# Where seven Strassen products stand between the tiles of second products in an attention, experts and MLP kernel

## The chip, the cores and the metric

The kernel runs on one core of a Trainium2 chip. The metric is the device time of one execution in microseconds; three runs of a kernel are timed and their median is compared. One further execution is recorded by the hardware profiler; its rows are in microseconds from the start of its span unless marked ns.

## The reference

Three layers follow each other on 1152 tokens of 512 features. First an attention (2 batches, 8 heads, 576 positions, head size 64) that adds a coarse softmax attention over groups of four positions to a local one over the seven nearest positions. Then a mixture of eight experts whose weights P come from a gate and eight Sinkhorn rounds. Then an MLP with a softplus.

```python
out_up = np.repeat(out_d, factor, axis=2)       # coarse attention
x = out_up + out_local                          # (1152, 512)
logits = x @ w_gate; P = np.exp(logits - logits.max())
for _ in range(8):                              # Sinkhorn
    P /= P.sum(1, keepdims=True) + 1e-09
    P /= P.sum(0, keepdims=True) + 1e-09
    P *= N / E
for e in range(8):                              # w1: 512x1024, w2: 1024x512
    out += P[:, e:e+1] * (np.maximum(x @ w1[e], 0) @ w2[e])
h = out @ w_in                                  # 512 x 2048
return (np.maximum(h, 0) + np.log1p(np.exp(-np.abs(h)))) @ w_out
```

## The kernel before, in words

The MLP is treated as two more experts, so there are ten (`NE`), numbered 0 to 9. Tokens are split in two sets: s=0 holds 512 (four tiles of 128, halves of 256), s=1 holds 640 (five tiles, halves of 320). An expert's hidden width is cut in four pairs of 128-row blocks (`p`). One step is one expert, one token set and one `p`; there are 80 steps, listed in `steps`. Steps 0 to 3 run beside the attention, steps 4 to 79 afterwards in the main loop (line 792).

**First products.** `first(n)` computes a step's hidden values by a Strassen scheme: seven products (lines 623 to 648) in the order 4, 0, 2, 5, 1, 3, 6 instead of eight. All arithmetic is fp32 split in a high and a low part (`xh`, `xl`, `w1h`, `w1l`), so each product is six matmuls (line 601) of 256 or 320 columns. Products 4, 2, 1 and 6 use one PSUM bank in turn, products 0 and 3 share a second bank, product 5 has a third, which is the first bank of the next step. Therefore product 2 waits until ScalarE has copied product 4 out (`t1`, line 610), product 1 until product 2 is copied (`u2`), product 6 until VectorE has added product 1 into `c22` (line 615), and the next step's product 5 until the hidden values of product 6 (`hh` by ScalarE, line 558, and `hl` by VectorE, line 559, both read from the bank) are made. In the MLP steps the hidden values take a longer chain (lines 563 to 575).

**Second products.** `second(n, ...)` multiplies one token tile of the hidden values with `w2`: six matmuls of 512 columns (line 660) into the tile's own PSUM bank. After the last step of a group, `weigh` (line 677) adds the bank into `acc` on VectorE.

**Order of the work.** TensorE's order is the order in which the program emits its instructions (`manual_schedule`). The other engines' orders are planned by a list scheduler from the same program. In the usual step n of the main loop the seven products of step n+2 (`ahead[n] == [n + 2]`) are shared out ahead of the tiles of second products of step n. With four tiles the shares are 2, 2, 2, 1, with five tiles 2, 2, 1, 1, 1. Of the 76 steps of the main loop 68 are usual ones (4 to 57 and 64 to 77): 30 have four tiles and 38 five. Around the turn from experts to MLP (58 to 63) other shares hold, and the last two steps have no products.

**What else hangs on the order.** `lead(n)` calls `fetch_first` once a weight block has been used for the last time: after product 6 its buffers are refilled, with two DMAs into `raw` (issued on SyncE), casts on ScalarE (lines 132 and 138), sums on GpSimd (line 111) and low parts on VectorE and GpSimd (lines 133 and 139). For experts 1 to 6 this is the case in each four-tile step: 24 times. For the MLP's blocks the refill is two DMAs alone. `used(n)` does the same for `w2` after the last tile. `convert` (32 pieces, from step 12) turns the MLP's float64 weights into split fp32 on VectorE, ScalarE and GpSimd. Up to step 8 a piece of the Sinkhorn rounds (`next(balance)`) follows each tile but the first; every second one begins with a small matmul (line 509) that waits for VectorE.

Of the kernel before, what the change touches and what calls it, by code (L numbers as in the profile page):

```python
# [20 lines left out]
def attention_moe_mlp(ctx: ExitStack, tc: tile.TileContext, q, k, v, w_gate, w1, w2, w_in, w_out, out):  # L21
# [3 lines left out]
    E, _, FF = w1.shape  # L25
# [26 lines left out]
    OPS = 7  # L52
# [481 lines left out]
    for e, g, s, p in steps:  # L534
        m = e * NP + p
# [114 lines left out]
    def outputs(s):  # L650
        return [bank(tag, "yps") for tag in ("at", "at", "at", "at", "y")[: len(TILES[s])]]

    def second(n, hh, hl, i, y, start, stop):
        s = steps[n][2]
        wh, wl = weights[uses[n]][1]
        tok = slice(i * P, (i + 1) * P)
        m = 0
        for f in range(2):
            for a, b in ((hh, wh), (hh, wl), (hl, wh)):
                nc.tensor.matmul(y, a[:, f, tok], b[:, f, :], start=(start and m == 0), stop=(stop and m == 5))  # L660
                m += 1
# [3 lines left out]
    def weigh(e, s, i, y):  # L665
        t, e = TILES[s][i], min(e, E)
        once = (e, t) not in seen
        seen.add((e, t))
        if e in (0, E) and once:
            acc[t] = rows[s].tile([P, DM], F32, tag="row", name="acc")  # L670
            (nc.vector.tensor_copy if i % 2 else nc.scalar.copy)(acc[t], y)
        elif e in (0, E):
            nc.vector.tensor_tensor(acc[t], y, acc[t], op=ALU.add)  # L673
        else:
            if e == 1 and once:
                nc.gpsimd.tensor_tensor(acc[t], acc[t], pr[:, t, 0:1].to_broadcast([P, DM]), op=ALU.mult)
            nc.vector.scalar_tensor_tensor(  # L677
                out=acc[t], in0=y, scalar=pr[:, t, e : e + 1], in1=acc[t], op0=ALU.mult, op1=ALU.add,
            )

    def again(s, banks):

        if s:
            xf = [pair("xf2") for _ in range(2)]
        else:
            xf = [rawp.tile([P, 2, 2 * HALF[s]], F32, tag="raw", name="xf2") for _ in range(2)]
        for i, t in enumerate(TILES[s]):
            tp = bank(banks, "tp")
            for kk in range(KD):
                nc.tensor.transpose(tp[:, kk * P : (kk + 1) * P], acc[t][:, kk * P : (kk + 1) * P], ident)  # L690
            tpv = tp.rearrange("p (a k c) -> p a k c", a=2, k=2)
            for kk in range(2):
                nc.scalar.copy(xf[kk][:, :, i * P : (i + 1) * P], tpv[:, :, kk])
            yield
            if s:
                yield
        for i in ORDER:
            for kk in range(2):
                yield from operands(s, kk, xf[kk], (i,), [nc.vector if i in FASTI else nc.gpsimd])

    def lead(n):
        yield from first(n)
        f = uses[n]
        if final[f] == n and f + 3 < len(fetches):
            fetch_first(f + 3, fetches[f + 3])

    def used(n):
        f = uses[n]
        if final[f] == n and f + 3 < len(fetches):
            fetch_second(f + 3, fetches[f + 3])  # L710
# [66 lines left out]
    ahead = {n: [n + 2] for n in range(BESIDE, len(steps) - 2)}  # L777
# [6 lines left out]
    def leading(ns):  # L784
        for n in ns:
            if steps[n][0] == E and n == (turned[1] if steps[n][2] else ends[E, 1] + 1):
                for _ in pending:
                    pass
            yield from lead(n)

    with tc.manual_schedule(engines={mybir.EngineType.PE}):
        for n in range(BESIDE, len(steps)):
            e, g, s, p = steps[n]
            if begins[n]:
                ys = outputs(s)
            hs = ready.pop(n)
            products = leading(ahead.get(n, []))
            left = OPS * len(ahead.get(n, []))
            if n == ends[E - 1, 0]:

                left -= len(TILES[0]) - 1

            half = [i for i in range(len(ys)) if (i + 1) * P > HALF[s]]
            half = half[1:] + half[:1] if HALF[s] % P else half
            tiles = half + [i for i in range(len(ys)) if i not in half]
            for m, i in enumerate(tiles):
                for _ in range(-(-left // (len(tiles) - m))):
                    next(products)
                    left -= 1
                second(n, *hs, i, ys[i], begins[n], stops[n])  # L810
                if stops[n]:
                    weigh(e, s, i, ys[i])
                if m:
                    next(balance, None)
                for _ in range(PIECES):
                    if pending:
                        next(pending, None)
            if n == ends[E - 1, 0]:
                pending = again(0, "at")
                for _ in TILES[0]:  # L820
                    next(pending)
                    next(products, None)
            for _ in products:
                pass
            used(n)
            if n == ends[E - 1, 1]:
                pending = again(1, "y")
            elif n in (ends[NE - 1, 0], ends[NE - 1, 1]):
                for t in TILES[s]:
                    nc.sync.dma_start(out[t * P : (t + 1) * P, :], acc[t])  # L830
            while pieces < 2 * HALVES and n >= CV + pieces * 3 // 2:
                convert(pieces)
                pieces += 1
# [25 lines left out]
```

## Time and profile before

| what | value |
|---|---|
| three runs | 1096.89, 1097.08, 1092.58 us (median 1096.89) |
| the profiled execution | span 1094.7 us from the first to the last instruction; no other time of it is recorded |
| TensorE matmuls | busy 1060.0 us (97% of the span), 6385 matmuls |
| TensorE weight loads | busy 938.0 us (86%) |
| VectorE, ScalarE, GpSimd | busy 727.0 us (66%), 555.2 us (51%), 537.6 us (49%) |
| first products (line 601) | 3360 matmuls, mean records of 297 to 301 ns |
| second products (line 660) | 2160 matmuls |
| mean granted TensorE clock | 0.979 of 2.4 GHz |

Records of matmuls overlap: the engine starts the next while one runs, so the distance between two starts, and not the record's length, is what a matmul costs.

### The profile page before, as it was taken

The numbers are of one execution on the slowest core, as the hardware profiler recorded it, in microseconds if no ns is written. First come the engines' busy times: TensorE is split into PE (matmuls) and PEld (weight loads), VectorE is DVE, ScalarE is ACT, GpSimd is POOL, SyncE is SP. The second block draws the span as 40 slices with busy tenths as digits, with TensorE's granted clock in tenths as the row PEclk, the third lists the DMA queues.
The fourth block names the chain that finished last, engine by engine and source line by source line (L and its number), as shares of the span: only waits on it lengthen the run. The fifth ranks groups of instructions, "written<-read, shape, count | busy, mean of one in ns | idle before, by whom it ended". The sixth has DMA issues, their size and how long they took to land.

```text
span 1094.7 us, 17873 instructions
## 1 busy us (share of the span) xinstructions
PE 1060.0 (97%) x6385; PEld 938.0 (86%) x6385; DVE 727.0 (66%) x1532; ACT 555.2 (51%) x1443; POOL 537.6 (49%) x569
## 2 busy tenths in 40 slices
PE   6899999999999999999999999999999998999998
PEld 5678888998987889888888988898898897889987
DVE  6889665565666676667657665766663578766765
ACT  4667645343444444434444443444443567676763
POOL 6735235464467676756766455354664212222321
PEclk9579999999999999999999999999999999999999
DMA  8454101111235334434443332223333273244112
GB/s 175 118 115 109 49 27 55 62 58 40 84 100 145 115 110 143 132 105 127 122 134 102 117 112 93 100 93 110 102 116 116 106 278 139 113 175 182 68 39 87
DMA packets 133497, 119.70 MB, mean 109 GB/s; under 512 B 35744, under 2 KB 111776, under 8 KB 133408
## 3 DMA queue, kind: packets, MB, share of 16 engines
q1 hardware_dynamic: 133408, 118.56, 35.0%
q8 instruction: 50, 0.82, 0.3%
q14 instruction: 39, 0.32, 0.1%
HBM read 93.11 MB, written 25.43 MB: 108 GB/s over the span
## 4 chain that ended last, share of the span: by engine, by line
PE 40%; POOL 5%; DMA 5%; DVE 3%; issue 2%; ACT 2%; SPq 0%; POOLq 0%; ACTq 0%; DVEq 0%
PE yps L660 21%; PE m L601 19%; DMA raw<-in_moe_w_out 2%; POOL sums L111 2%; POOL w2l L154 1%; POOL cva L188 1%; POOL cva L197 1%; DMA raw<-in_moe_w 1%; DMA raw<-in_moe_w_in 1%; DVE cva L178 1%; POOL w1l L139 1%; DVE cva L189 0%; DVE cva L179 0%; DVE cva L182 0%; DMA s_out<-cva 0%
## 5 line engine op out<-in xcount | busy, mean ns | idle before, releaser
L601 PE MATMUL m<-xh,w1h 128*128 128x320 f32 (+1 forms) x1120 | 336.6, 301 | 13.1 <-ACT t L610 6.3
L601 PE MATMUL m<-xh,w1l 128*128 128x320 f32 (+1 forms) x1120 | 332.5, 297 | 0.0
L601 PE MATMUL m<-xl,w1h 128*128 128x320 f32 (+1 forms) x1120 | 332.4, 297 | 0.0
L601 PEld LDWEIGHTS m<-xh,w1h 128*128 128x128 f32 x1120 | 212.2, 189 | 38.7 <-ACT t L610 10.8
L601 PEld LDWEIGHTS m<-xl,w1h 128*128 128x128 f32 x1120 | 212.4, 190 | 11.8
L601 PEld LDWEIGHTS m<-xh,w1l 128*128 128x128 f32 x1120 | 212.2, 190 | 0.2 <-issue 0.2
L660 PE MATMUL yps<-w2h,hh 128*128 128x512 f32 x502 | 198.5, 395 | 0.0
L660 PE MATMUL yps<-w2l,hh 128*128 128x512 f32 x502 | 198.4, 395 | 0.0
L660 PE MATMUL yps<-w2h,hl 128*128 128x512 f32 x502 | 195.5, 389 | 0.0
L660 PE MATMUL yps<-w2h,h 128*128 128x512 f32 x436 | 153.3, 393 | 0.0
L615 DVE TENSOR_TENSOR c<-m,t 128x256 f32<-128x256 f32 (+1 forms) x160 | 72.3, 452 | 100.9 <-PE m L601 99.5
L139 POOL TENSOR_TENSOR w1l<-sums,w1h 128x512 fp32r<-128x512 f32 x72 | 95.8, 1345 | 78.2 <-ACT w1h L138 54.4
L571 POOL TENSOR_TENSOR ab<-ab,up 128x320 f32<-128x320 f32 (+1 forms) x64 | 53.9, 843 | 157.2 <-ACT ln L567 109.8
L154 POOL TENSOR_TENSOR w2l<-raw,w2h 128x512 fp32r<-128x512 f32 x72 | 94.9, 1339 | 71.4 <-ACT w2h L153 71.3
L558 ACT ACTIVATE hh<-c 128x256 fp32r<-128x256 f32 (+1 forms) x138 | 60.0, 443 | 125.0 <-DVE c L615 123.3
L559 DVE SCALAR_TENSOR_TENSOR hl<-c,hh 128x256 fp32r<-128x256 f32 (+1 forms) x138 | 91.4, 668 | 35.0 <-ACT hh L558 33.2
L660 PEld LDWEIGHTS yps<-w2h,hl 128*128 128x128 f32 x502 | 94.4, 188 | 21.3
L677 DVE SCALAR_TENSOR_TENSOR acc<-yps,pr,acc 128x512 f32<-128x512 f32 x117 | 86.9, 743 | 29.5 <-PE yps L660 29.4
L660 PEld LDWEIGHTS yps<-w2h,hh 128*128 128x128 f32 x502 | 94.7, 189 | 12.6 <-DVE acc L673 0.2
L660 PEld LDWEIGHTS yps<-w2l,hh 128*128 128x128 f32 x502 | 94.7, 189 | 11.1 <-issue 0.4
L660 PEld LDWEIGHTS yps<-w2h,h 128*128 128x128 f32 x436 | 82.6, 189 | 14.8
L188 POOL TENSOR_TENSOR cva<-cva,raw 128x512 uint32<-128x512 uint32 x32 | 42.7, 1336 | 95.2 <-DVE raw L185 76.6
(134 smaller groups left out, 1700.7 us busy)
## 6 DMA issues: line engine op xcount, KB each, us to landing
raw<-in_moe_w SPq DMA_DIRECT2D x72, 256.0 KB
raw<-in_moe_w SPq DMA_DIRECT2D x36, 512.0 KB
w1h<-s_in SPq DMA_DIRECT2D x10, 896.0 KB
w1l<-s_in SPq DMA_DIRECT2D x10, 896.0 KB
raw<-in_moe_w_in SPq DMA_DIRECT2D x32, 256.0 KB
raw<-in_moe_w_out SPq DMA_DIRECT2D x16, 512.0 KB
w2l<-s_out SPq DMA_DIRECT2D x10, 512.0 KB
w2h<-s_out SPq DMA_DIRECT2D x10, 512.0 KB
```

The costliest lines, as they stand in the source:

```text
L111: nc.gpsimd.tensor_tensor(sums[i], a, b, op=op)
L139: nc.gpsimd.tensor_tensor(lo[:, part], sums, hi[:, part].bitcast(F32), op=ALU.subtract)
L154: nc.gpsimd.tensor_tensor(lo[:, i], raw[:, i], hi[:, i].bitcast(F32), op=ALU.subtract)
L178: nc.vector.tensor_scalar(a, high, 0x07FFFFFF, 3, op0=ALU.bitwise_and, op1=ALU.logical_shift_left)
L188: nc.gpsimd.tensor_tensor(a, a, low, op=ALU.add)
L558: nc.scalar.activation(hh, c, AF.Relu)
L559: nc.vector.scalar_tensor_tensor(out=hl, in0=c, scalar=0.0, in1=hh.bitcast(F32), op0=ALU.max, op1=ALU.subtract)
L571: nc.gpsimd.tensor_tensor(ab, ab, up, op=ALU.subtract)
L601: nc.tensor.matmul(b[:, :h], x[:, i, kk, :], y[s][:, i, kk, :], start=(not more and n == 0), stop=(n == 5), skip_group_check=more,)
L615: nc.vector.tensor_tensor(c, b[:, :h], t, op=ALU.add)
L660: nc.tensor.matmul(y, a[:, f, tok], b[:, f, :], start=(start and m == 0), stop=(stop and m == 5))
L677: nc.vector.scalar_tensor_tensor(out=acc[t], in0=y, scalar=pr[:, t, e : e + 1], in1=acc[t], op0=ALU.mult, op1=ALU.add,)
```

## The change

In the 68 usual steps the shares are written down: 2, 2, 2, 0 for four tiles, 2, 2, 0, 2, 0 for five. That leaves one of the seven products, which the loop that empties the generator behind the tiles (`for _ in products`) emits. So product 6 of step n+2 now follows the last second product of step n, and products 4 and 0 of step n+3 follow it directly. In five-tile steps products 1 and 3 stand together ahead of the fourth tile.

```diff
+    SHARES = {4: (2, 2, 2, 0), 5: (2, 2, 0, 2, 0)}
...
+            spaced = left == OPS and ahead.get(n) == [n + 2]
             for m, i in enumerate(tiles):
-                for _ in range(-(-left // (len(tiles) - m))):
+                share = -(-left // (len(tiles) - m))
+                if spaced:
+                    share = SHARES[len(tiles)][m]
+                for _ in range(share):
                     next(products)
                     left -= 1
                 second(n, *hs, i, ys[i], begins[n], stops[n])
```

With Y for the six matmuls of one tile, TensorE's order in a four-tile step is 4 0 Y 2 5 Y 1 3 Y 6 Y before and 4 0 Y 2 5 Y 1 3 Y Y 6 after; in a five-tile step 4 0 Y 2 5 Y 1 Y 3 Y 6 Y before and 4 0 Y 2 5 Y Y 1 3 Y Y 6 after.

## Rows read from the trace of the kernel before

**Rows 1.** Head of the page: the span.
```profile
span 1094.7 us, 17873 instructions
```

**Rows 2.** Waits of weight loads, then matmuls: total, times, longest (us).
```profile
PEld m L601 <- ACT t L610: 10.8, 11, 2.9
PEld m L601 <- DVE c L615: 6.8, 12, 1.5
...
PEld m L601 <- ACT u L610: 4.4, 6, 1.2
...
PEld m L601 <- DVE hl L559: 2.8, 4, 0.9
...
PE m L601 <- DVE c L615: 2.4, 3, 1.0
```

**Rows 3.** Windows: the MLP stretch; busy time and count of each engine, granted clock.
```profile
940.00:1079.00 139.00, 139.00 (x827) 125.17 (x826) 94.82 (x236) 97.98 (x247) 38.62 (x48) 1.00 0.31 118
```

**Rows 4.** Timeline, weight loads: start, length, what, in brackets idle before and releaser.
```profile
332.29 0.19 PEld L601 LDWEIGHTS m<-xh,w1h 128*128 128x128 f32 x1 [0.57 <-DVE c L615]
...
338.83 0.19 PEld L601 LDWEIGHTS m<-xh,w1h 128*128 128x128 f32 x1 [1.29 <-ACT t L610]
...
346.40 0.19 PEld L601 LDWEIGHTS m<-xh,w1h 128*128 128x128 f32 x1 [1.44 <-DVE c L615]
...
352.86 0.19 PEld L601 LDWEIGHTS m<-xh,w1h 128*128 128x128 f32 x1 [0.62 <-DVE hl L559]
...
383.22 0.19 PEld L601 LDWEIGHTS m<-xh,w1h 128*128 128x128 f32 x1 [0.54 <-DVE c L615]
...
454.53 0.19 PEld L601 LDWEIGHTS m<-xh,w1h 128*128 128x128 f32 x1 [0.15 <-DVE c L615]
...
492.70 0.19 PEld L601 LDWEIGHTS m<-xh,w1h 128*128 128x128 f32 x1 [1.46 <-DVE c L615]
...
705.84 0.19 PEld L601 LDWEIGHTS m<-xh,w1h 128*128 128x128 f32 x1 [0.85 <-ACT u L610]
...
780.85 0.19 PEld L601 LDWEIGHTS m<-xh,w1h 128*128 128x128 f32 x1 [0.38 <-DVE c L615]
```

**Rows 5.** Chain of waits around 880 and 1077: start, length, what.
```profile
874.26 1.43 PE m L601 x12
...
879.18 2.87 PE m L601 x24
...
1076.64 1.39 PE yps L660 x6
...
1078.74 12.28 PE yps L660 x54
```

**Rows 6.** Timeline, matmuls, a Sinkhorn matmul in step 4.
```profile
185.07 0.40 PE L660 MATMUL yps<-w2h,hl 128*128 128x512 f32 x1
185.93 0.41 PE L509 MATMUL m<-pr,ones 128*128 128x72 f32 x2 [0.46 <-DVE pr L506]
```

**Rows 7.** Timeline, ScalarE, behind product 6 of step 23.
```profile
396.24 0.93 ACT L132 CAST w1h<-raw 128x256 fp32r<-128x256 f32 x2 [0.39 <-PE m L601]
397.07 0.62 ACT L138 CAST w1h<-sums 128x512 fp32r<-128x512 f32 x1
397.60 0.43 ACT L558 ACTIVATE hh<-m 128x320 fp32r<-128x320 f32 x1
397.92 0.61 ACT L138 CAST w1h<-sums 128x512 fp32r<-128x512 f32 x1
398.54 0.37 ACT L610 COPY t<-m 128x256 f32<-128x256 f32 x1
```

**Rows 8.** Timeline, VectorE, the same stretch.
```profile
397.77 2.12 DVE L133 TENSOR_TENSOR w1l<-raw,w1h 128x256 fp32r<-128x256 f32 x2
...
400.47 0.47 DVE L559 SCALAR_TENSOR_TENSOR hl<-m,hh 128x320 fp32r<-128x320 f32 x1
```

**Rows 9.** Timeline, matmuls: the first of product 5 of step 24.
```profile
401.11 0.28 PE L601 MATMUL m<-xh,w1h 128*128 128x256 f32 x1
```

## The prediction

> **What bounds the kernel now.** I read the page first. TensorE is the busiest engine by far, and its records cover nearly the whole span of 1094.7 us [rows 1]. Then the windows: in the MLP's usual steps TensorE is busy for 139.00 of 139.00 us at the full clock of 2.4 GHz [rows 3]. An order that leaves the same matmuls can gain there only in the distances between matmuls, not in waits. Elsewhere there are waits, and the view of waits names them. Weight loads of first products waited 10.8 us for ScalarE's copies t, 6.8 for VectorE's sums c, 4.4 for the copies u and 2.8 for hl [rows 2]: 24.8 us in all. That is the whole purse for this change, and it is too large: a loading stands idle for a while ahead of any product, the smallest case listed being 0.15 us [rows 4], and some of the waits lie in the turn from experts to MLP, whose shares stay. The matmuls' own rows give the other end, 2.4 us for c where the loads show 6.8 [rows 2], because a matmul's record outlasts its turn and hides part of a wait.
>
> Last I followed the waits on the timeline. In the code product 2 is the one that needs t, product 1 needs u, product 6 needs c22, and product 5 of the next step needs hl. So the four rows of the waits are four places in the order, and each can be asked: does the new order put more or less work of TensorE between the making and the use?
>
> **Product 6, waiting for c.** In four-tile steps it stood one product and one tile behind product 1; now one product and two tiles. A tile is 1.39 us [rows 5], and the longest wait listed is 1.46 [rows 4]. So these waits nearly vanish. Gross size: 6.8 us less twelve times 0.15, that is 5.0 (bounds 2.4 and 6.8) [rows 2, 4]. But it isn't all kept. The waits at 332.29, 346.40 and 492.70 make 0.57 + 1.44 + 1.46, less 0.45 for the usual idle: 3.0 us [rows 4]. Behind the first TensorE waits again for t at 338.83 (1.29), behind the second for hl at 352.86 (0.62), and the third repeats the second [rows 4]. There ScalarE and VectorE are late by themselves, with refills and conversions in their queues; a TensorE that comes earlier waits longer at the next place. I count those 3.0 us as given back. Of the other 2.0 I take 1.6, since one of the twelve (about 0.4) is not ahead of product 6 of a usual step; these run from 383.22 (0.54) to 780.85 (0.38), six of size [rows 4]. Term: -1.6 us.
>
> **Product 1, waiting for u.** In five-tile steps it gets one more tile behind product 2. One wait lies there, at 705.84, 0.85 us [rows 4], less 0.15: -0.7 us. In four-tile steps nothing changes for it.
>
> **Products 4 and 2.** Product 2 stays one product and one tile behind product 4, so its waits for t, the largest of the four (10.8 us, [rows 2]), are not helped. What comes onto ScalarE ahead of the copy t may change; see the new waits.
>
> **Sinkhorn.** In step 4 a small matmul starts at 185.93, 0.86 us behind the last matmul of a tile at 185.07, where 0.23 is usual (a sixth of 1.39); it waits for VectorE [rows 5, 6]. The piece that begins this chain now has two products and a tile ahead of the matmul instead of one product and a tile. Term: -0.6 us, bounds 0 and -0.6.
>
> **Neighbours.** The chain shows that a tile of second products behind a product costs 1.39 us. Of the nine tiles in the 12.28 us from 1078.74 the first stands behind a product and eight behind a tile: (12.28 - 1.39) / 8 = 1.361 [rows 5]. So 0.026 to 0.03 us are saved for each tile that follows a tile. There is one such tile in each of 30 four-tile steps and two in each of 38 five-tile steps, 106 in all: -2.7 to -3.0 us; I take the lower. For products it goes the other way: twelve matmuls of 256 columns cost 1.43 and 24 in one run 2.87 [rows 5], so up to 0.01 us is lost when two runs become one. That happens 106 times too (30 + 2 x 38); at half of that bound it is +0.6. Term: -2.1 us, bounds -3.0 and +1.1. It holds in all 68 steps, the MLP's included.
>
> The Trainium skill's page "TensorE: Matmul & The Clock Gate", section "Back-to-back issue gap", gives a warm gap of N/2.4 + 2.5 ns, which depends on the columns alone; it would be 216 ns for 512 columns, and the neighbour would cost nothing. The rows show 232 and 227 ns (1.39 and 1.361 over six) [rows 5], so the trace disagrees in size and in the neighbour. By that rule this term would be 0 and the sum -1.7 us.
>
> **New waits.** Three products in a row (6, then the next step's 4 and 0) leave ScalarE and VectorE less time between product 6 and the next step's products 2 and 5: one tile less, 1.39 us. Usually that is covered. In refill steps it may not be. Behind product 6 of step 23, at 396.24, ScalarE does 0.93 of casts, 0.62, 0.43 for hh, 0.61, and its copy t ends at 398.91, 2.67 us after the product [rows 7]. The new deadline of product 2 is half of 2.87, plus a tile, 2.82: just held. VectorE ends hl at 400.94, 4.70 us after the product [rows 8], behind two w1l of 2.12. Product 5 started at 401.11, 4.87 after [rows 9]; a tile earlier is 3.48. So it would wait 1.2 us. I take this once: +1.2. The low bound is 0, if VectorE's plan puts hl ahead of w1l. The high one is 24 refill steps of 1.2, 29 us, if all were like this one; only four waits for hl, 2.8 us in all, are listed now [rows 2], so I stay near the low end.
>
> **What is moved without a price.** The refill of w1 begins behind product 6, so its DMA issues on SyncE and its casts come a tile later in each usual step. The block is wanted three blocks on, several steps later, each of at least seven products and four tiles; the sums from raw on GpSimd do not wait for product 6. Without that cover the cost would be the 1.39 us of the tile. DMA issues queued behind on SyncE come as much later under the same cover. The last weigh of a group now stands ahead of product 6 on VectorE; the bank it frees is wanted one or more tiles and three products later. In the MLP steps the chain of product 6 on ScalarE now meets t; nothing waits there [rows 3], and I put 0.
>
> **Sum.** -1.6 - 0.7 - 0.6 - 2.1 + 1.2 = -3.8 us: the profiled execution would go from 1094.7 to 1090.9. The median of the runs is 1096.9, 2.2 above that span, and the lowest run 1092.6 is 2.1 under it; I subtract from the median: 1093.1 us. A measurement of this kernel tells about 0.5%, 5.5 us, from no change, so this is no change that can be seen, on the fast side.
>
> **Rivals.** First, nothing is given back, and the new waits don't come: -5.0 - 0.7 - 0.6 - 2.1 = -8.4, 1088.5 us. For it: the two engines are far from full, so lateness in one place could be caught up by a tile of slack. Against it: the pairs of waits six microseconds apart [rows 4].
>
> Second, slower: ScalarE's and VectorE's plans put the refill (w1h, w1l) ahead of t and hl in the short stretch behind product 6. Its place is the 24 refill steps, its price 1.2 us a step as worked out for step 23. It outweighs the gains and the bound of 5.5 us from 9.3 / 1.2, eight further steps, on; with twelve the time is 1093.1 + 14.4 = 1107 us. For it: such a plan is in the trace [rows 7, 8]. Against it: only four waits for hl are listed [rows 2]. The skill's page "PSUM — Partial Sum Buffer", section "Engine vs sequencer instructions", says that the queues of these engines are strict first-in first-out, which is how one cast would hold up a copy; the rows agree, as t follows the casts without a gap.
>
> Third, the change doesn't do what it says: the neighbour saving belongs to the quiet end of the kernel, and waits only move. Then -1.7 us or less remains, about 1095.5 us.
>
> **How the numbers follow.** The forecast has 0.47, with a range of its own of 1089 to 1098; the first rival 0.22; the second 0.16; the third 0.15. Faster by over 0.5% is below 1091.4: all of the first rival and a fifth of the forecast, 0.31. Slower is above 1102.4: the second rival, 0.16. The rest, 0.53, is no change. The range runs from 1087 (the first rival with 1.4 us of the waits for t, too) to 1103 (eight steps of the second rival) and leaves about 0.2 out.
>
> **What would show it.** Right: waits of weight loads for c fall from 6.8 to under 3 us; the chain shows tiles behind tiles at 1.36 also in the middle of the kernel; the small matmul of step 4 starts without a wait; waits for hl rise to about 4 to 6 us. Wrong: waits for t above 14 or for hl above 8 us would make it slower; waits for t that fall below 7 would make it faster than forecast, and I have no term for that. A plan of ScalarE and VectorE that differs in more places than behind product 6 is what would most likely break the sum.

## The result and the profile after

The changed kernel takes 1108.34 us (median of 6 runs, 1106.50 to 1111.68) beside 1096.20 us for the kernel before on the same chip (6 runs, 1092.58 to 1098.39). The ratio is 1.0114, with a 95% interval of 1.0089 to 1.0139: about 12 us slower. The prediction said 1093.1 us and a range of 1087 to 1103. It was wrong, and on the wrong side.

The head of the page after, where the span answers to [rows 1]:

```profile
span 1106.4 us, 17875 instructions
PE 1063.2 (96%) x6385; PEld 940.6 (85%) x6385; DVE 745.1 (67%) x1532; ACT 549.4 (50%) x1443; POOL 539.8 (49%) x569
```

The span is 11.7 us longer, with the same 6385 matmuls. TensorE is busy 3.2 us longer (1063.2 us beside 1060.0), so the other 8.5 us are in gaps. VectorE is busy 18.1 us longer than the 727.0 us of before, though the change gave it no work. That is the first hint where to look. The waits after, to be read against [rows 2] (total, times, longest, in us):

```profile
PEld m L601 <- ACT t L610: 17.9, 18, 3.6
PEld m L601 <- DVE c L615: 8.5, 12, 1.6
...
PEld m L601 <- DVE hl L559: 5.4, 4, 1.8
PEld m L601 <- ACT u L610: 4.0, 4, 1.4
```

One more line of that view, outside these, has 1.4 us for the hidden values in the other buffer (h, also line 559):

```profile
PEld m L601 <- DVE h L559: 1.4, 2, 0.9
```

Against before, the waits for t grew by 7.1 us, for hl and h by 4.0, for c by 1.7, and for u shrank by 0.4: 12.4 us more in all. These are sums over the whole span. The change acts only in the main loop, and the product that opens it in both orders (product 4 of step 4) starts at different times in the two traces, before (first) and after (second):

```profile
147.84 0.45 PE L601 MATMUL m<-xh,w1h 128*128 128x320 f32 x2
```

```profile
146.56 0.45 PE L601 MATMUL m<-xh,w1h 128*128 128x320 f32 x2
```

So 1.3 us of the after trace are gained ahead of the main loop, where the order is the same, and from there on the new order needs 12.9 us more: 959.8 us beside 946.9.

The waits for c should have nearly gone. The timeline of weight loads shows where they are now, in the form of [rows 4]:

```profile
326.96 0.19 PEld L601 LDWEIGHTS m<-xh,w1h 128*128 128x128 f32 x1 [1.80 <-DVE hl L559]
350.56 0.19 PEld L601 LDWEIGHTS m<-xh,w1h 128*128 128x128 f32 x1 [1.63 <-ACT t L610]
352.21 0.19 PEld L601 LDWEIGHTS m<-xh,w1h 128*128 128x128 f32 x1 [0.88 <-DVE hl L559]
...
474.70 0.19 PEld L601 LDWEIGHTS m<-xh,w1h 128*128 128x128 f32 x1 [1.81 <-DVE hl L559]
...
616.64 0.19 PEld L601 LDWEIGHTS m<-xh,w1h 128*128 128x128 f32 x1 [1.60 <-DVE c L615]
...
659.57 0.29 PEld L601 LDWEIGHTS m<-xh,w1h 128*128 128x128 f32 x1 [3.60 <-ACT t L610]
...
831.39 0.19 PEld L601 LDWEIGHTS m<-xh,w1h 128*128 128x128 f32 x1 [1.39 <-DVE c L615]
...
942.48 0.19 PEld L601 LDWEIGHTS m<-xh,w1h 128*128 128x128 f32 x1 [2.32 <-ACT t L610]
```

The two large waits for c ahead of product 6 in four-tile steps, at 346.40 and 492.70 in [rows 4], have no counterpart; in fact no four-tile step has a wait of over 0.3 us there any more, where before nine had, 5.9 us in all. But the next step's product 2 (350.56) and product 5 (352.21) wait instead, and waits for c appear ahead of product 6 in five-tile steps (616.64, 831.39), which had none of that size: ten now, 7.0 us in all. What TensorE waits for at 326.96, 474.70, 616.64 and 831.39 stands directly behind operations of a conversion piece (lines 178 to 197) on VectorE. At 659.57 only hh stands between such an operation and the copy t. At 350.56 hh and two casts of a refill do, and behind the same two casts VectorE makes the two w1l that 352.21 waits for; those casts came late, behind a piece's cast that had waited 1.89 us for GpSimd. 942.48 lies at the beginning of the MLP's steps (below). ScalarE ahead of 350.56:

```profile
348.47 0.62 ACT L196 CAST raw<-sums 128x512 fp32r<-128x512 f32 x1 [1.89 <-POOL sums L111]
```

The worst is the one at 659.57, ahead of product 2 of step 45. ScalarE's timeline before it:

```profile
653.85 0.42 ACT L558 ACTIVATE hh<-c 128x256 fp32r<-128x256 f32 x1
654.18 1.13 ACT L153 CAST w2h<-raw 128x512 fp32r<-128x512 f32 x2
658.36 0.62 ACT L196 CAST raw<-cva 128x512 fp32r<-128x512 f32 x1 [3.06 <-DVE cva L189]
658.88 0.38 ACT L558 ACTIVATE hh<-m 128x256 fp32r<-128x256 f32 x1
659.16 0.64 ACT L610 COPY t<-m 128x256 f32<-128x256 f32 x2
```

ScalarE stands idle for 3.06 us in front of a cast of the conversion that waits for VectorE (line 189), and behind that cast stand hh and the copy t, which TensorE wants. VectorE and GpSimd in the same stretch:

```profile
653.74 2.86 DVE L559 SCALAR_TENSOR_TENSOR hl<-c,hh 128x256 fp32r<-128x256 f32 x2
656.52 1.75 DVE L189 SCALAR_TENSOR_TENSOR cva<-raw,cva 128x512 f32<-128x512 f32 x1
```

```profile
653.57 1.31 POOL L188 TENSOR_TENSOR cva<-cva,raw 128x512 uint32<-128x512 uint32 x1 [3.75 <-DVE raw L185]
654.86 2.86 POOL L154 TENSOR_TENSOR w2l<-raw,w2h 128x512 fp32r<-128x512 f32 x2
659.05 1.27 POOL L197 TENSOR_TENSOR cva<-cva,raw 128x512 fp32r<-128x512 f32 x1 [1.33 <-ACT raw L196]
```

Two hl take 2.86 us there and the operation of line 189 takes 1.75, while GpSimd works without a break from 653.57 to 657.72. In the kernel before the same piece goes as follows, on ScalarE, VectorE and GpSimd. ScalarE does the cast of line 196 ahead of the refill of w2 (line 153), so GpSimd reaches line 154 only when VectorE is through.

```profile
650.25 0.62 ACT L196 CAST raw<-cva 128x512 fp32r<-128x512 f32 x1 [1.14 <-DVE cva L189]
...
651.10 1.14 ACT L153 CAST w2h<-raw 128x512 fp32r<-128x512 f32 x2
```

```profile
649.53 0.69 DVE L189 SCALAR_TENSOR_TENSOR cva<-raw,cva 128x512 f32<-128x512 f32 x1 [0.86 <-POOL cva L188]
650.14 0.42 DVE L559 SCALAR_TENSOR_TENSOR hl<-c,hh 128x256 fp32r<-128x256 f32 x1
```

```profile
648.08 1.42 POOL L188 TENSOR_TENSOR cva<-cva,raw 128x512 uint32<-128x512 uint32 x1 [3.95 <-DVE raw L185]
650.95 1.30 POOL L197 TENSOR_TENSOR cva<-cva,raw 128x512 fp32r<-128x512 f32 x1 [1.46 <-ACT raw L196]
652.21 2.54 POOL L154 TENSOR_TENSOR w2l<-raw,w2h 128x512 fp32r<-128x512 f32 x2
```

That wait cost more than itself. The windows around it (the column behind the busy times is TensorE's granted clock) show 1.2 GHz for 6.8 us:

```profile
658.50:665.30 6.80, 5.72 (x20) 5.05 (x21) 2.13 (x5) 2.09 (x6) 1.27 (x1) 0.50 0.68 224
665.30:672.00 6.70, 6.70 (x41) 6.00 (x40) 5.90 (x12) 2.38 (x5) 1.20 (x1) 1.00 0.03 10
```

From the end of the wait at 659.57 to 665.30 TensorE works for 5.73 us at half the clock and so loses half of that, 2.9 us. Each of the two main loops has one more stretch at 0.50, after from 167.0 to 170.4 us and before from 916.3 to 919.7; they are equally long, so about 1.7 us on each side stand against each other.

The gains are there as well. The first matmuls of two tiles, of the product behind them, and the small matmul of step 4 (compare [rows 5, 6]):

```profile
560.84 0.40 PE L660 MATMUL yps<-w2h,hh 128*128 128x512 f32 x1
...
562.22 0.39 PE L660 MATMUL yps<-w2h,hh 128*128 128x512 f32 x1
...
563.58 0.28 PE L601 MATMUL m<-xh,w1h 128*128 128x256 f32 x1
```

```profile
184.56 0.39 PE L660 MATMUL yps<-w2h,hl 128*128 128x512 f32 x1
184.79 0.34 PE L509 MATMUL m<-pr,ones 128*128 128x72 f32 x2
```

The tile behind a product costs 1.38 us and the tile behind a tile 1.36, in the middle of the kernel. The small matmul follows its predecessor after 0.23 us and waits for nothing; two steps later 0.3 of the 0.7 us that this saves are lost again, in a new wait for t (0.41 us at 203.79).

### The profile page after: what moved, and what is told of

Same layout as the page of the kernel before. It is cut to its first block, busy times and chain, and to the rows that moved or that the text cites. A ratio compares the mean times of both kernels' runs of the same rounds, so it can differ in the third digit from the quotient of the medians.

```text
span 1106.4 us, 17875 instructions
## 1 busy us (share of the span) xinstructions
PE 1063.2 (96%) x6385; PEld 940.6 (85%) x6385; DVE 745.1 (67%) x1532; ACT 549.4 (50%) x1443; POOL 539.8 (49%) x569
## 4 chain that ended last, share of the span: by engine, by line
PE 61%; DVE 14%; POOL 9%; DMA 7%; issue 4%; ACT 3%; SPq 1%; POOLq 0%; DVEq 0%; ACTq 0%
PE yps L660 29%; PE m L601 26%; POOL sums L111 3%; DMA raw<-in_moe_w 2%; DMA raw<-in_moe_w_out 2%; POOL w2l L154 2%; DMA raw<-in_moe_w_in 2%; DVE cva L178 1%; PE sc L368 1%; POOL cva L197 1%; DVE cva L189 1%; POOL w1l L139 1%; DVE cva L182 1%; DVE acc L677 1%; DVE c L615 1%
## 5 line engine op out<-in xcount | busy, mean ns | idle before, releaser
L601 PE MATMUL m<-xh,w1h 128*128 128x320 f32 (+1 forms) x1120 | 337.8, 302 | 23.6 <-ACT t L610 11.7
L601 PEld LDWEIGHTS m<-xh,w1h 128*128 128x128 f32 x1120 | 212.8, 190 | 46.5 <-ACT t L610 17.9
L660 PE MATMUL yps<-w2h,h 128*128 128x512 f32 x436 | 147.0, 391 | 0.0
L154 POOL TENSOR_TENSOR w2l<-raw,w2h 128x512 fp32r<-128x512 f32 x72 | 98.0, 1382 | 84.0 <-ACT w2h L153 84.0
L677 DVE SCALAR_TENSOR_TENSOR acc<-yps,pr,acc 128x512 f32<-128x512 f32 x117 | 85.9, 743 | 17.7 <-PE yps L660 17.4
L660 PE MATMUL yps<-w2l,h 128*128 128x512 f32 x218 | 85.6, 393 | 0.0
```

Of the source, the lines that this page charges most:

```text
L154: nc.gpsimd.tensor_tensor(lo[:, i], raw[:, i], hi[:, i].bitcast(F32), op=ALU.subtract)
L601: nc.tensor.matmul(b[:, :h], x[:, i, kk, :], y[s][:, i, kk, :], start=(not more and n == 0), stop=(n == 5), skip_group_check=more,)
L677: nc.vector.scalar_tensor_tensor(out=acc[t], in0=y, scalar=pr[:, t, e : e + 1], in1=acc[t], op0=ALU.mult, op1=ALU.add,)
```

## The experiments

Two theories stood against each other first. One is the prediction's second rival: the refill of w1 in the shorter stretch behind product 6 holds up t and hl (theory A in the expectations). The other is that the conversion pieces do so (B), which the prediction had named only in passing. A third (C) is that products 1 and 3 together crowd VectorE in five-tile steps. Later ones took the second apart.

**Which part of the order.** The four-tile shares alone, the five-tile shares alone, and for five tiles the pair of products 1 and 3 alone, or the last product alone:

```diff
-    SHARES = {4: (2, 2, 2, 0), 5: (2, 2, 0, 2, 0)}
+    SHARES = {4: (2, 2, 2, 0), 5: (2, 2, 1, 1, 1)}    # e1_four
+    SHARES = {4: (2, 2, 2, 1), 5: (2, 2, 0, 2, 0)}    # e2_five
+    SHARES = {4: (2, 2, 2, 1), 5: (2, 2, 0, 2, 1)}    # e11_five_pair
+    SHARES = {4: (2, 2, 2, 1), 5: (2, 2, 1, 1, 0)}    # e12_five_last
```

> Shares 2, 2, 2, 0 in the 30 four-tile steps, five-tile steps as before (2, 2, 1, 1, 1). Theory A (the stretch behind product 6 is a tile shorter, and in the 24 refill steps the casts and low parts of w1 stand ahead of t and hl there): most of the loss is here, 1104 to 1110 us. Theory B (pieces of the conversion, planned for an earlier time than they can run at, stand ahead of t, c22 and hl in the queues of ScalarE and VectorE; where they collide is changed by any new order): no share of the loss is fixed, anything from 1092 to 1106 us. Theory C (products 1 and 3 together crowd VectorE in five-tile steps): 1093 to 1097 us.

> Shares 2, 2, 0, 2, 0 in the 38 five-tile steps, four-tile steps as before (2, 2, 2, 1). Theory A: no refill follows these product 6, so 1093 to 1097 us. Theory B: anything from 1092 to 1106 us, and the difference to before does not add up with that of the four-tile edit to the 12 us of the whole change. Theory C: most of the loss, 1103 to 1110 us.

> Five-tile shares 2, 2, 0, 2, 1: products 1 and 3 together, product 6 stays ahead of the last tile; four-tile steps as before. If the tile taken from behind product 6 is what the five-tile edit costs: 1094 to 1098 us. If the pair of products 1 and 3 is (VectorE gets c22 and c12 at once, and product 6 has a tile less behind product 1): 1100 to 1107 us, with waits for c above 8 us.

> Five-tile shares 2, 2, 1, 1, 0: only product 6 moves behind the last tile; four-tile steps as before. If the tile behind product 6 is the cost: 1100 to 1107 us, with waits for t near 18 us. If the pair is: 1094 to 1098 us.

| kernel | median us | ratio to before, 95% | waits for t | c | hl |
|---|---|---|---|---|---|
| e1_four | 1101.50 | 1.0045, 1.0030 to 1.0060 | 17.4 | 3.8 | 3.4 |
| e2_five | 1105.18 | 1.0084, 1.0051 to 1.0116 | 18.7 | 6.2 | 2.8 |
| e11_five_pair | 1097.83 | 1.0027, 1.0013 to 1.0040 | 8.6 | 14.8 | 2.0 |
| e12_five_last | 1101.61 | 1.0054, 1.0029 to 1.0078 | 15.8 | 2.6 | 3.7 |

Each of the three that move product 6 raises the waits for t from 10.8 to between 15.8 and 18.7 and lowers those for c; the pair, which leaves product 6 in its place, does the opposite and costs 0.3% (1 to 4 us). So most of the price hangs on product 6, in steps of both kinds, and it is paid at t; the four-tile and the five-tile part, 4.7 and 8.4 us over the 1096.8 of before in that comparison, make up the whole 12. That they add up is not what theory B expected. The time of e2_five is the one that theory C asked for, but the pair alone costs only 1.9 us, so C is at most a small part. In e1_four c fell by 3.0 us (6.8 to 3.8), and t took more than twice that.

**Without the conversion pieces.** Of the 32 pieces 28 are left out, so the MLP works with its first converted block throughout; the same in both kernels.

```diff
-                convert(pieces)
+                if pieces in (0, 1, HALVES, HALVES + NP):
+                    convert(pieces)
```

> The kernel before with 4 of the 32 conversion pieces; the other 28 are left out, and the MLP uses the first converted block of each kind in all places, with the same DMAs from scratch. Theory B: the waits of product 2 for t and of product 6 for c in experts 2 to 6 go, 1080 to 1088 us. Theory A says little of this kernel alone: 1080 to 1095 us.

> The changed kernel with the same 28 conversion pieces left out. Theory A: still 8 to 12 us above the kernel before with them left out, since the refills are all there. Theory B: 2 to 4 us below it (tiles next to tiles, the waits for c), since only the collisions with pieces made the loss. Theory C: 8 to 12 us above, the products being the same.

The old order takes 1081.51 us and the new one 1079.53 (ratios to the kernel before 0.9862, 0.9841 to 0.9883, and 0.9851, 0.9830 to 0.9871). The 2.0 us between them are no clear gain: each interval is about 2 us wide on either side, and in the two traces the difference lies ahead of the main loop, which takes 933.5 us in the old order and 933.6 in the new one. What is clear is that the loss is gone. The refills of w1 are all still there, 24 of them, in the same short stretch. The waits for t are 5.3 us in the old order and, in the new one,

```profile
PEld m L601 <- ACT t L610: 5.6, 6, 2.9
```

That fells the second rival in the form that the prediction gave it. The refills alone cost next to nothing; nearly all of the loss needs the pieces. The pieces left out also take their DMAs and buffers with them; that it is their operations that count is for the next experiments.

**Luck of the plan.** Perhaps the pieces only fall on bad steps, or the planner puts them ahead by a wrong order of importance. All pieces a step later (`CV = 13`), and the copies, sums and hidden values planned with high priority:

```diff
-    CV = 12
+    CV = 13                          # e5_after_cv13, e6_before_cv13
...
+            with tc.high_priority():    # e9_after_prio, e10_before_prio: around t, u, c, hh, hl
```

> The changed kernel with all conversion pieces one step later (CV = 13). Theory B in its strict form, B1 (a piece collides where the planned order of the queues happens to put it ahead of t, c22 or hl; the step at which pieces begin decides where): the time moves by 2 to 8 us either way from 1108, and its distance to the kernel before with the same shift is not 12 us but anything from -4 to +16. Form B2 (with pieces in the queues the new order lacks room wherever they stand, above all the tile less behind product 6): 1105 to 1111 us and a distance of 9 to 14 us.

> The kernel before with all conversion pieces one step later. B1: 1090 to 1106 us, not the same as 1096.5. B2: within 2 us of 1096.5, since the old order has the room.

> The changed kernel with the steps' own operations (t, u, c, hh, hl) given a higher priority in the planner than refills and conversion pieces. Theory B3 (the lateness is an order of the queues: a piece or a refill stands ahead of t, hl or c22 because it came earlier in the program): waits for t, c and hl fall from 33 us in all to below 20, 1094 to 1100 us. Rival B4 (it is the load of VectorE in the short stretch, whatever the order): 1105 to 1112 us, waits as before.

> The kernel before with the same priority. B3: waits fall from 25 us to 15 or so, 1088 to 1095 us. B4: 1093 to 1099 us.

With the pieces a step later the old order stays at 1095.13 us (0.9993, 0.9979 to 1.0007) and the new one takes 1103.95 (1.0068, 1.0048 to 1.0088): still 9 us apart, 3 less than as changed, which the intervals allow to be chance. So most of the loss is no accident of the step at which the pieces begin. With high priority the times are 1096.19 us (1.0006, 0.9992 to 1.0021) and 1107.73 (1.0123, 1.0097 to 1.0149), and the waits for t in the latter are 17.6. But the priorities hardly moved the plan. In order of time ScalarE's operations in e9_after_prio differ from those of the changed kernel in 6 of 1443 places, VectorE's in 14 of 1532 and GpSimd's in none, and the cast of line 196 waits 3.06 us ahead of t as before. So these two runs don't say whether queues with t, c and hl ahead of the pieces would save the loss: that rival, a matter of the plan alone, remains untested.

**Casts and sign off ScalarE.** The casts of line 196 and the absolute value of line 186 are made on VectorE, so that nothing of the conversion stands ahead of t on ScalarE, at the price of some 50 to 60 us more on VectorE (784.6 us busy in the old order, 794.2 in the new):

```diff
-        nc.scalar.activation(high.bitcast(F32), high.bitcast(F32), AF.Abs)
+        nc.vector.tensor_scalar(high, high, 0x7FFFFFFF, None, op0=ALU.bitwise_and)
...
-            nc.scalar.copy(hi, x)
+            nc.vector.tensor_copy(hi, x)
```

> The changed kernel with the pieces' absolute value and casts (lines 186 and 196) on VectorE in place of ScalarE, so no operation of a piece stands in ScalarE's queue. B1 and B2 if the piece's cast ahead of t is what holds product 2 up: weight loads' waits for t fall from 17.9 to 5 to 9 us (the refills and the turn stay), the long one near 658 us and the fall of the clock there go, 1098 to 1104 us. If VectorE is the late one (its multiply of line 189 waits for GpSimd, and c22 and hl stand behind): waits for c and hl rise instead, 1106 to 1115 us.

> The kernel before with the same two operations on VectorE. If the cast ahead of t is what costs: waits for t fall from 10.8 to 3 to 7 us, 1091 to 1096 us. If VectorE is the late one: 1097 to 1105 us.

The old order takes 1118.43 us (1.0213, 1.0184 to 1.0241), the new one 1133.89 (1.0344, 1.0328 to 1.0359). The waits of weight loads, new order (e7_after_dve):

```profile
PEld m L601 <- DVE hl L559: 20.4, 14, 3.0
PEld m L601 <- DVE c L615: 15.6, 14, 3.1
PEld m L601 <- DVE h L559: 9.8, 6, 2.7
PEld m L601 <- ACT t L610: 8.5, 7, 2.8
```

and old order (e8_before_dve):

```profile
PEld m L601 <- DVE c L615: 29.0, 21, 3.0
PEld m L601 <- ACT t L610: 8.6, 7, 2.9
PEld m L601 <- DVE hl L559: 2.9, 4, 1.1
```

Both times lie above all that was expected. Two things are to be seen. The waits for t fall from 17.9 to 8.5 us, the same as in the old order, as they should if the conversion's operations in ScalarE's queue held t up. It is no proof alone, since TensorE now waits 45.8 us for VectorE in place of 15.3, and ScalarE gains time meanwhile; the rows at 658.36 and 348.47 show it for single waits. And a VectorE made late shows where each order has its room. The old one has a tile behind product 6, so hl is in time (2.9 us) and c is late (29.0). The new one has given that tile to the stretch ahead of product 6: c halves, and hl and h, 2.9 in the old order, come to 30.2. The change moves room from one deadline to another.

**VectorE's load or the chain through GpSimd.** Two of a piece's five VectorE operations are left out (lines 179 to 184, the last bits of the mantissa and the sign), or GpSimd's add of the rounding bit is (line 188), so that line 189 no longer waits for GpSimd:

```diff
-        nc.vector.scalar_tensor_tensor(
-            out=a, in0=low, scalar=29, in1=a, op0=ALU.logical_shift_right, op1=ALU.bitwise_or
-        )
-        nc.vector.scalar_tensor_tensor(
-            out=a, in0=high, scalar=0xC0000000, in1=a, op0=ALU.bitwise_and, op1=ALU.bitwise_or
-        )
...
-        nc.gpsimd.tensor_tensor(a, a, low, op=ALU.add)
```

> The changed kernel with two of the five VectorE operations of each conversion piece left out (the two that put the mantissa's last bits and the sign into the word; some 48 us of VectorE in all; the second expert weights are not exact any more). VectorE's-load theory: the pieces cost the changed kernel time because VectorE is late with c and hl behind them, so with these operations gone the changed kernel stands at most 3 us above the kernel before treated alike, and its waits for t fall from 17.9 to 8 to 12 us. Chain-through-GpSimd theory (the casts on ScalarE wait for the operation behind GpSimd's sum, and t stands behind the casts): the difference stays 8 to 14 us.

> The kernel before with the same two operations of each piece left out. VectorE's-load theory: 1088 to 1092 us, as c at product 6 comes earlier in the steps with a piece. Chain-through-GpSimd theory: 1093 to 1096 us, as nothing that it waits for has moved.

> The changed kernel with GpSimd's add of the rounding bit left out of each piece (some 43 us of GpSimd; the converted weights are truncated, not rounded). Chain-through-GpSimd theory: the operation behind it no longer waits for GpSimd, so the cast comes early, the waits for t fall from 17.9 to 8 to 12 us and the kernel stands at most 3 us above the kernel before treated alike. VectorE's-load theory: the load is the same, the difference stays 8 to 14 us.

> The kernel before with the same add left out. Chain-through-GpSimd theory: 1093 to 1096 us, waits for c as before. VectorE's-load theory: the same to 1 us; up to 3 us less if VectorE's operations are stretched by GpSimd's work beside them.

Lighter on VectorE: new order 1097.23 us (1.0025, 0.9989 to 1.0061), old order 1092.05 (0.9976, 0.9958 to 0.9993), 5.2 us apart instead of 12, with intervals of about 4 and 2 us on the two. Lighter on GpSimd: 1105.26 (1.0103, 1.0076 to 1.0130) and 1094.17 (0.9990, 0.9972 to 1.0008), 11.1 us apart. In the new order the waits for t are 13.8 us in the first case and 22.6 in the second:

```profile
PEld m L601 <- ACT t L610: 13.8, 11, 3.0
```

```profile
PEld m L601 <- ACT t L610: 22.6, 15, 3.3
```

The wait for GpSimd's add is not the cause by itself: without it that theory asked for 3 us or less, and the interval of the difference is about 8 to 15 us. The load theory asked for 3 us or less and for 8 to 12 us of waits for t; it got 5.2, with an interval of about 1 to 10 us, and 13.8. By the medians VectorE's part of the piece counts for more, but the profiled executions don't bear it out. They took 1100.40 and 1093.80 us in the first case, 6.6 apart, and 1100.12 and 1092.71 in the second, 7.4 apart; that of the new order was 3 us above its median in the first and 5 us under it in the second, so the 22.6 us of waits belong to a fast execution. How much either part of a piece costs is not settled.

**Less on VectorE, and the order where no piece runs.** Low parts of refilled weights on GpSimd; and the new order only before step 12 and from step 60 on:

```diff
-            nc.vector.tensor_tensor(lo[:, part], src, hi[:, part].bitcast(F32), op=ALU.subtract)
+            (nc.gpsimd if f > 2 else nc.vector).tensor_tensor(lo[:, part], src, hi[:, part].bitcast(F32), op=ALU.subtract)
...
-            spaced = left == OPS and ahead.get(n) == [n + 2]
+            spaced = left == OPS and ahead.get(n) == [n + 2] and not 12 <= n < 60
```

> The changed kernel with the low parts of the refilled weights (from the fourth set on) made on GpSimd in VectorE's place. VectorE's-load theory: with some 40 to 55 us less on VectorE, 3 to 7 us faster than the changed kernel, so 1101 to 1105 us. The rival: GpSimd is slower at it and stretches VectorE's operations beside it, weights come later, and the kernel stays at 1108 us or goes above it.

> The order of the changed kernel only in the steps beside which no conversion piece runs (before step 12 and from step 60 on), the order before in steps 12 to 59. VectorE's-load theory: the gains stay (neighbours and Sinkhorn stretch) and the new waits do not come: 1 to 2.5 us faster than before, ratio 0.9975 to 0.999. A theory by which the refills in the short stretch cost time: 3 to 6 us slower, as about half of the refill steps still have the new order.

The first is a miss, and a useful one: 1113.03 us (1.0153, 1.0139 to 1.0167), 5 us above the changed kernel, as its rival had it. VectorE's busy time did fall, from 745.1 to 702.2 us, but GpSimd's rose from 539.8 to 599.9, and the waits for t grew:

```profile
PEld m L601 <- ACT t L610: 26.6, 25, 2.9
```

VectorE's load as a sum is therefore not the cause. Nor do the 5 us more lie in the main loop: in the trace product 4 of step 4 starts at 150.71 us, 4.2 later than after, and from there on the two differ by 0.8 us. What matters is probably when a piece's chain, VectorE to GpSimd to VectorE to ScalarE, is through. The group of line 189 on VectorE shows that more work on GpSimd delays it, after (first) and in e18_after_lowpool (second; busy, mean ns, idle before):

```profile
L189 DVE SCALAR_TENSOR_TENSOR cva<-raw,cva 128x512 f32<-128x512 f32 x32 | 26.2, 819 | 10.4 <-POOL cva L188 10.2
```

```profile
L189 DVE SCALAR_TENSOR_TENSOR cva<-raw,cva 128x512 f32<-128x512 f32 x32 | 30.2, 944 | 12.5 <-POOL cva L188 12.5
```

The same operation takes 819 ns on the average in the one and 944 in the other, and 0.69 us at 649.53 (above), where GpSimd is idle.

The second is also a miss: 1097.72 us (1.0006, 0.9994 to 1.0018), no gain, where 1 to 2.5 us were expected. It does show that without the new order in steps 12 to 59 the 12 us are gone. The largest loss is at the beginning of the MLP's steps, ahead of product 2 of step 67, in a stretch that still has the new order. Weight loads there, before and in e17_free_steps:

```profile
930.46 0.19 PEld L601 LDWEIGHTS m<-xh,w1h 128*128 128x128 f32 x1 [0.47 <-ACT t L610]
```

```profile
931.96 0.19 PEld L601 LDWEIGHTS m<-xh,w1h 128*128 128x128 f32 x1 [2.31 <-ACT t L610]
```

The wait is 1.8 us longer, and the changed kernel has it too (2.32 at 942.48, shown above). It is a second place at which a tile less behind product 6 bares a late t, with no piece near: there ScalarE has the MLP's chain (lines 563 to 575) to do. From product 4 of step 66 to that of step 68 e16_before_plight takes 30.86 us and e15_after_plight 32.43, both at the full clock there: 1.6 us for the new order. No complete version here is shown to beat the kernel before. One that was not run is the new order before step 12 and from step 68 on alone.

## Why the prediction was wrong

**Right.** *Neighbours*: 1.38 and 1.36 us for the two tiles, in the middle of the kernel. Where nothing waits, from product 4 of step 69 to that of step 79, the new order takes 115.33 us and the old one 115.60; 0.27 us in ten steps are some 1.9 in 68 (an estimate), beside a term of -2.1. The 216 ns that the prediction takes from the Trainium skill's page "TensorE: Matmul & The Clock Gate", section "Back-to-back issue gap", are there the gap of an isolated matmul, and the page has about 131 ns for a stream of loads and matmuls; the trace agrees with neither, at 227 to 230 ns. *Sinkhorn*: the small matmul no longer waits, though of 0.7 us only 0.4 are kept. *Product 6, waiting for c* is right in kind for four-tile steps, where all waits over 0.3 us are gone (5.9 us; e1_four has -3.0 in all, where the term had -1.6). *Product 1*: the wait at 705.84 is gone, but a new one of 1.22 us stands at 825.65, so that u gained 0.4 in place of 0.7.

**The step that failed is *New waits*.** It took +1.2 us, from bounds of 0 and 29, and stayed near the low end because few waits for hl were listed [rows 2]. The runs showed +11.1 in its place: 7.1 for t and 4.0 for hl and h. Behind it come 2.9 us of halved clock, which had no term. In the main loop alone the balance of all waits is 13.0 us, since one of the waits for hl before (0.87 us at 98.71) and some smaller ones lie ahead of it. With -2.1 and -0.6 that makes 13.0 + 2.9 - 2.1 - 0.6 = 13.2, beside the 12.9 by which the main loop grew.

Two choices inside that step went wrong. First, it priced the refill, on the example of step 23 [rows 7 to 9]. In the trace after that very place has no wait. VectorE does only 1.01 us of w1l ahead of hl there, and ends it at 399.21:

```profile
397.80 1.01 DVE L133 TENSOR_TENSOR w1l<-raw,w1h 128x256 fp32r<-128x256 f32 x2
398.73 0.48 DVE L559 SCALAR_TENSOR_TENSOR hl<-m,hh 128x320 fp32r<-128x320 f32 x1
```

It was mostly the conversion pieces that lay ahead of t and hl, and they come two steps in three, not in 24 steps. Two w1l directly ahead of hl or h, as the prediction had it, do make TensorE wait at four places (300.63, 352.21, 448.35, 499.59: 3.2 us), but each time their casts had come behind a piece's cast that waited 1.3 to 1.9 us for GpSimd. Operations of the pieces stood directly ahead of c and u in waits of before, at 346.40 and 705.84 [rows 4]; the waits behind 346.40 were read as lateness that is "given back", and not as a sign of a chain that a tile of room covers in most other steps. Second, the low end was taken from the number of waits listed. A view of waits tells what is late now. It doesn't tell how much of the 1.39 us of a tile is used up in the steps without a wait, and that is what the change took away. The prediction's allowance of 0.15 us for a load that doesn't wait was a misreading as well: 0.15 is the smallest case that the list shows, and between its waits a load follows a tile after 0.04 us (412.06 to 412.10 before). That made its gross size for c 5.0 us where some 6.3 were meant, and is not what failed.

***Products 4 and 2*** said that the waits for t "are not helped", as the distance from product 4 to product 2 stays. The distance did stay; but t is a place in ScalarE's queue and not only a matter of product 4. Behind product 6 that queue holds hh and a cast that waits for VectorE, and it now has one tile less until product 2. The Trainium skill's page "PSUM — Partial Sum Buffer", section "Engine vs sequencer instructions", says that ScalarE, VectorE and GpSimd work their queues strictly first in, first out; the trace agrees, as t starts 0.80 us after the start of a cast that waited 3.06, with only hh between.

***Product 6, waiting for c*** had no part for five-tile steps, and there new waits came: c rose by 1.7 us in all. Product 6 kept its distance from product 1 there, but the pair of products 1 and 3 alone raises the waits for c to 14.8 us (e11_five_pair), and at 616.64 and 831.39 operations of a piece stand ahead of c on VectorE.

**What is moved without a price** put 0 for the MLP's steps, because nothing waits from 940 us on [rows 3]. The MLP's steps 66 and 67 lie ahead of that window, and there the new order costs 1.6 us.

**The rivals.** The second one had the right side, the right place (the stretch behind product 6) and nearly the right time, 1107 us. Its mechanism was the refill, and e4_after_noconv shows that refills alone cost next to nothing, so that the time was near is luck. The prediction's own sign for "wrong", waits for t above 14 us, is what came.

**What is shown, and what is argued.** Shown: nearly all of the loss needs the pieces, and some 1.6 us come at the MLP's beginning without them; it comes with product 6; at the longest wait t is held up by a conversion's cast on ScalarE that waits for VectorE; less work on VectorE in sum doesn't shorten the main loop. Argued: that the other waits for t in steps with a piece come the same way. By the medians alone, taking work off VectorE in the pieces about halves the loss. Open: how it divides between VectorE and the chain, as the intervals of e13 and e14 leave their difference anywhere between about 1 and 10 us; whether another order of the queues would avoid it; and why the plan puts ScalarE's w2 casts ahead of the piece's cast near 655 us after and behind it before.

## What to carry to other kernels

A tile of work moved ahead of one product is taken from behind it: ask of every engine queue, not only of the operand named, what stands in it during the stretch that gets shorter, and what that in turn waits for. A wait list prices gains well and losses badly, since it holds nothing of the slack that is about to be used. Take an occasional side job (here a conversion in 32 pieces) out in both versions: that tells in two runs whether the order or its company costs the time. And where a run is to test an order of queues, see in its trace that the order has changed.

## What the runs showed of the hardware

VectorE's operations on two tensors in SBUF take longer beside GpSimd. Line 189 took 0.69 us alone and 1.75 where GpSimd was at work until 657.72, and two hl, of which one takes 0.42 us alone, took 2.86 together. The Trainium skill's page "SBUF — State Buffer", section "SBUF: two separate sides", says that such a VectorE operation and a GpSimd operation shut each other out for a whole instruction. The trace agrees to about 0.15 us: 657.72 and 0.69 give 658.41, and line 189 ended at 658.27.

During a gap of 3.60 us ahead of one product the granted clock fell to 1.2 GHz and stayed there for 6.8 us, so TensorE lost 2.9 us more behind the gap. A single long wait can weigh more than its length. It doesn't always: ahead of product 2 of step 66 the two orders wait 2.85 and 2.87 us, and behind the first the clock is 0.50 from 916.3 to 919.7 us, behind the second it stays at 1.00.
